# Two inputs transposed by the DMA crossbar, attention in four groups of four heads, and part of its sums as identity matmuls

## The chip, the cores and the metric

The kernel runs on one core of a Trainium2 chip. The time is device microseconds of one execution; where several runs are given, their median is meant. A profile is one execution recorded by the hardware profiler: TensorE (PE, with its weight loads shown apart as PEld), VectorE (DVE), ScalarE (ACT), GpSimd (POOL), SyncE (SP), and the DMA queues. Each engine executes its own list of instructions; semaphores join the lists.

## What is computed

Two independent layers on two inputs of 2048 tokens by 448 features, in bf16, written side by side into one output of 2048 x 896.

```python
# A: a diagonal complex state-space layer, 448 states
Lam_bar = jnp.exp(dt * Lam)
B_bar = ((Lam_bar - 1.0) / Lam)[:, None] * Bmat
Bu = jnp.einsum("bld,pd->blp", x + 0j, B_bar)
for t in range(L):
    h = Lam_bar[None, :] * h + Bu[:, t, :]
y = 2.0 * jnp.einsum("blp,dp->bld", hseq, Cmat).real + x * Dskip[None, None, :]

# B: attention, 16 heads of 28, each token over 8 earlier tokens at distance 0, 2, ... 14
qkv = (x @ wqkv)                      # 448 -> 3 x 16 x 28
logits = jnp.einsum("bhsd,bhswd->bhsw", q, kg) * scale   # -1e9 before the first token
attn = softmax(logits)
o = jnp.einsum("bhsw,bhswd->bhsd", attn, vg)
out_b = o @ wo
```

## The kernel before

A token is 16 p + j: partition p holds 16 consecutive tokens j. So a window reaches at most 14 tokens back, into the partition above; `kd` and `vd` therefore have a halo of 14 tokens in front, filled by a DMA that shifts the last 14 tokens of every partition by one partition (`_halo`, L100).

Part B. `loads` (L54) brings the weights and x in token order. `prep` (L68) reorders the weights on DVE to (d, head) and transposes x on PE, four 128x112 blocks for each j, with a copy on ACT. `qk_proj` and `v_proj` (L104, L115) make k, q and v for all 16 heads: 48 PSUM tiles of 448 columns, four matmuls each; DVE empties k and q, ACT empties v. `attention` (L122) works on all heads at once, on DVE. For each of the eight distances w it multiplies q with the shifted k (7168 elements per partition) and adds over d in a tree of six further additions; softmax follows on 2048 elements per partition; for the values, eight multiplications by the weight and seven additions, done for tokens 0 to 11 and then 12 to 15 (`PV_SPLIT`). `tail` (L175) transposes the result on PE, copies it on DVE, multiplies by wo on PE, copies on ACT and stores from SP, one j at a time.

Part A. `setup` (L254) builds on DVE and ACT the powers of the diagonal, and on POOL the small matrices that apply them: `Mmat` (7 instructions), `Lmat`, `Pmat` (5) and `Gdiag`, in that order. `setup_weights` (L367) makes `Bcat`, the input matrix, by matmuls with `Gdiag`. `main` (L406) transposes x like part B and then has three stages. First level: 16 steps over j, each with 28 matmuls of x and 14 of the former state (`Lmat`), two ACT copies and a store of the state `ht` to `hs` in DRAM. Doubling: seven steps `l2A`, `l2B` across partitions, then `gaA`, `gaB`. Correction and output: for each j the state is read back (`hin`), corrected in PSUM (`coA`, `coB`, 14 matmuls), copied by ACT to `ht`, multiplied by `Ccat` and `Dg` into `y_ps`, copied and stored.

The order on each engine comes from a scheduler in the program's build: it gives every instruction the priority of its place in the program and simulates which is ready, with buffers taken from pools. The program's order is: parameters, loads, `b.prep`, `a.setup`, `b.qk_proj`, `b.v_proj`, `a.setup_c`, `a.setup_weights`, `b.loads2`, `a.main`, `b.attention`. PSUM has six buffers of tag `mm` (projections, all of part A, wo) and two of tag `pt` (transposes). All DMAs but the k halo (ACT) are issued from SP. The list is fixed when the program is built.

Of the kernel before, what the change touches and what calls it, by code (L numbers as in the profile page):

```python
# [9 lines left out]
ACT = mybir.ActivationFunctionType  # L10
ALU = mybir.AluOpType
# [5 lines left out]
D = 448  # L17
T = 16
# [27 lines left out]

class PartB:

    def __init__(self, tc, B_x, B_wqkv, B_wo, out_b, ident, pool, psum):
        self.tc, self.nc = tc, tc.nc  # L50
        self.B_x, self.B_wqkv, self.B_wo, self.out_b = B_x, B_wqkv, B_wo, out_b
        self.ident, self.pool, self.psum = ident, pool, psum

    def loads(self):  # L54
        nc, pool = self.nc, self.pool
        self.wn = pool.tile([KP, KT, 3 * D], bf16, name="wqkv_nat", tag="prod")
        nc.sync.dma_start(self.wn[:], self.B_wqkv.rearrange("(k p) c -> p k c", p=KP))
        self.x_sb = pool.tile([NCH, T, D], bf16, name="xb_sb", tag="xin")
        nc.sync.dma_start(self.x_sb[:], self.B_x[0].rearrange("(p j) d -> p j d", j=T))

    def loads2(self):
        nc, pool = self.nc, self.pool
        self.wo_p = pool.tile([KP, KT, D], bf16, name="wo_p")
        wo_v = self.B_wo.rearrange("(h kt dl) c -> dl h kt c", kt=KT, dl=7)
        for dl in range(7):
            nc.sync.dma_start(self.wo_p[dl * H:(dl + 1) * H, :, :], wo_v[dl])

    def prep(self):  # L68
        nc, pool, V = self.nc, self.pool, self.nc.vector
        self.wp = pool.tile([KP, KT * 3, DH, H], bf16, name="wqkv_p", tag="wp")  # L70
        wn_v = self.wn[:].rearrange("p k (w h d) -> p (k w) d h", w=3, h=H, d=DH)
        wpv = self.wp[:].rearrange("p (k w) d h -> p k w d h", w=3)
        wnv = wn_v.rearrange("p (k w) d h -> p k w d h", w=3)
        V.tensor_copy(wpv[:, :, 0:2], wnv[:, :, 0:2])
        V.tensor_copy(wpv[:, :, 2], wnv[:, :, 2])
        self.xT = pool.tile([KP, KT, T, NCH], bf16, name="xbT_sb", tag="xT")
        for j in range(T):
            pt = self.psum.tile([KP, KT, NCH], bf16, name="pt_x", tag="pt")
            for k in range(KT):
                nc.tensor.transpose(pt[:, k, :], self.x_sb[:, j, k * KP:(k + 1) * KP], self.ident[:])  # L80
            nc.scalar.copy(self.xT[:, :, j, :], pt[:])  # L81
        self.qd = pool.tile([NCH, DH, T, H], bf16, name="qd", tag="qd")
        self.kd = pool.tile([NCH, DH, TJ, H], bf16, name="kd", tag="kd")
        self.vd = pool.tile([NCH, DH, TJ, H], bf16, name="vd", tag="vd")
        zsrc = pool.tile([1, HALO * H], bf16, name="zsrc")
        nc.vector.memset(zsrc[:], 0.0)
        for t_ in (self.kd, self.vd):
            nc.sync.dma_start(t_[0:1, :, 0:HALO, :].rearrange("o d j h -> o d (j h)"),
                              zsrc[:].unsqueeze(1).to_broadcast([1, DH, HALO * H]))

    def _proj(self, j, which):
        nc = self.nc
        ps = self.psum.tile([NCH, DH, H], f32, name="qkv_ps", tag="mm")
        for k in range(KT):
            nc.tensor.matmul(ps[:].rearrange("p d h -> p (d h)"), lhsT=self.xT[:, k, j, :],  # L95
                             rhs=self.wp[:, k * 3 + which].rearrange("p d h -> p (d h)"),
                             start=(k == 0), stop=(k == KT - 1))
        return ps

    def _halo(self, t_, eng):  # L100
        eng.dma_start(t_[1:113, :, 0:HALO, :], t_[0:112, :, T:T + HALO, :])
        eng.dma_start(t_[113:128, :, 0:HALO, :], t_[112:127, :, T:T + HALO, :])

    def qk_proj(self):  # L104
        nc, V = self.nc, self.nc.vector
        scale = DH ** -0.5
        for j in range(T):
            ps = self._proj(j, 1)
            V.tensor_copy(self.kd[:, :, HALO + j, :], ps[:])
        self._halo(self.kd, nc.scalar)  # L110
        for j in range(T):
            ps = self._proj(j, 0)
            V.tensor_scalar(self.qd[:, :, j, :], ps[:], scale, None, op0=ALU.mult)  # L113

    def v_proj(self):  # L115
        nc, V = self.nc, self.nc.vector
        for j in range(T):
            ps = self._proj(j, 2)
            nc.scalar.copy(self.vd[:, :, HALO + j, :], ps[:])  # L119
        self._halo(self.vd, nc.sync)  # L120

    def attention(self):  # L122
        nc, pool, V = self.nc, self.pool, self.nc.vector
        qd, kd, vd = self.qd, self.kd, self.vd
        logits = pool.tile([NCH, W, JH], f32, name="logits", tag="wp")
        for w in range(W):
            off = HALO - DIL * w
            pr = pool.tile([NCH, DH, JH], bf16, name="prod", tag="prod")
            V.tensor_tensor(pr[:], qd[:].rearrange("p d j h -> p d (j h)"),  # L129
                            kd[:, :, off:off + T, :].rearrange("p d j h -> p d (j h)"), op=ALU.mult)  # L130
            V.tensor_tensor(pr[:, 0:14], pr[:, 0:14], pr[:, 14:28], op=ALU.add)  # L131
            V.tensor_tensor(pr[:, 0:7], pr[:, 0:7], pr[:, 7:14], op=ALU.add)
            V.tensor_tensor(pr[:, 0:3], pr[:, 0:3], pr[:, 3:6], op=ALU.add)
            V.tensor_tensor(pr[:, 0:1], pr[:, 0:1], pr[:, 1:2], op=ALU.add)
            V.tensor_tensor(pr[:, 2:3], pr[:, 2:3], pr[:, 6:7], op=ALU.add)
            V.tensor_tensor(logits[:, w, :], pr[:, 0, :], pr[:, 2, :], op=ALU.add)
            if w > 0:
                V.memset(logits[0:1, w, 0:DIL * w * H], -1e9)
        mx = pool.tile([NCH, 4, JH], f32, name="mx", tag="mx")
        V.tensor_tensor(mx[:], logits[:, 0:4, :], logits[:, 4:8, :], op=ALU.max)  # L140
        V.tensor_tensor(mx[:, 0:2], mx[:, 0:2], mx[:, 2:4], op=ALU.max)
        V.tensor_tensor(mx[:, 0:1], mx[:, 0:1], mx[:, 1:2], op=ALU.max)
        V.tensor_tensor(logits[:], logits[:], mx[:, 0:1, :].to_broadcast([NCH, W, JH]), op=ALU.subtract)
        nc.scalar.activation(logits[:], logits[:], ACT.Exp)
        sm = pool.tile([NCH, 4, JH], f32, name="sm", tag="mx")
        V.tensor_tensor(sm[:], logits[:, 0:4, :], logits[:, 4:8, :], op=ALU.add)
        V.tensor_tensor(sm[:, 0:2], sm[:, 0:2], sm[:, 2:4], op=ALU.add)
        V.tensor_tensor(sm[:, 0:1], sm[:, 0:1], sm[:, 1:2], op=ALU.add)
        V.reciprocal(sm[:, 1, :], sm[:, 0, :])
        attn = pool.tile([NCH, W, JH], bf16, name="attn", tag="attn")  # L150
        V.tensor_tensor(attn[:], logits[:], sm[:, 1:2, :].to_broadcast([NCH, W, JH]), op=ALU.mult)
        acc = pool.tile([NCH, DH, T, H], bf16, name="acc", tag="xin")
        self.o_nat = pool.tile([NCH, T, DH, H], bf16, name="o_nat", tag="qd")
        attn4 = attn[:].rearrange("p w (j h) -> p w j h", h=H)
        for (j0, j1) in self.PV_SPLIT:
            n = j1 - j0
            for w in range(W):
                off = HALO - DIL * w
                vv = vd[:, :, off + j0:off + j1, :]
                aa = attn4[:, w:w + 1, j0:j1, :].to_broadcast([NCH, DH, n, H])  # L160
                if w == 0:
                    V.tensor_tensor(acc[:, :, j0:j1, :], aa, vv, op=ALU.mult)
                else:
                    tmp = pool.tile([NCH, DH, T, H], bf16, name="pv_tmp", tag="prod")
                    V.tensor_tensor(tmp[:, :, 0:n, :], aa, vv, op=ALU.mult)  # L165
                    if w < W - 1:
                        V.tensor_tensor(acc[:, :, j0:j1, :], acc[:, :, j0:j1, :], tmp[:, :, 0:n, :], op=ALU.add)  # L167
                    else:
                        V.tensor_tensor(self.o_nat[:, j0:j1].rearrange("p j d h -> p d j h"),  # L169
                                        acc[:, :, j0:j1, :], tmp[:, :, 0:n, :], op=ALU.add)  # L170
            self.tail(j0, j1)

    PV_SPLIT = ((0, 12), (12, 16))

    def tail(self, j0, j1):  # L175
        nc, pool = self.nc, self.pool
        if j0 == 0:
            self.oT = pool.tile([KP, KT, T, NCH], bf16, name="oT_sb", tag="xT")
# [385 lines left out]
```

## Time and profile before

| | us |
|---|---|
| time, median of 3 runs (lowest to highest) | 213.12 (212.28 to 213.27) |
| span of the profiled execution, first to last instruction | 211.4 |
| DVE busy | 181.0 (86%) |
| PE busy / weight loads | 160.4 (76%) / 117.4 |
| ACT busy | 100.2 (47%) |
| POOL busy | 28.1 (13%) |
| PE waits for x of part B | 18.5 |
| projections on PE, in the chain | 29.29 to 62.62 |
| part A: first level to the last output copy | 69 to 176.8 |

The span and the time are of different executions; the profiled execution's own time is its span and what lies around it, so a sum is made against the span and then carried over. A group's busy time counts all of its instructions; it is on the path only where another engine waits for it. The chain that ended last, followed back from the last instruction, gives the path: until 62.6 us it consists of the x load, transposes and projections, then of part A on PE until about 123 us, and from there to the end of attention on DVE with the last tail.

### The profile page before, as it was taken

The page shows a single profiled execution, that of the slowest core. Times are in us where ns is not written, and L with a number is a line of the kernel's source. Part 1 is how long each engine was busy: PE and PEld are TensorE (multiplying, and loading weights), DVE is VectorE, ACT ScalarE, POOL GpSimd, SP SyncE. Part 2 cuts the span into 40 slices and gives each one's busy share as a digit, 9 for nine tenths or more (in the row PEclk, how much of TensorE's full clock was granted, in tenths as well). Part 3 has the DMA queues.
Part 4 walks back from the last instruction along what each step waited for, and adds up shares of the span by engine and source line. Part 5 has one row for each costly group of instructions (what it writes and reads, how often), then busy time and mean ns, then how long its engine had stood idle before and what let it go on. Part 6 is the DMA issues. An engine that isn't in the chain of part 4 may idle for free.

```text
span 211.4 us, 4117 instructions
## 1 busy us (share of the span) xinstructions
PE 160.4 (76%) x1709; PEld 117.4 (56%) x1709; DVE 181.0 (86%) x197; ACT 100.2 (47%) x193; POOL 28.1 (13%) x35
## 2 busy tenths in 40 slices
PE   0004999999997799999995763998888883297773
PEld 0003765555567799999994652565555551154441
DVE  0359998888929999999999996999999999999950
ACT  2053792002689993344337796344455541024432
POOL 2000899991000000000000000000000000000000
PEclk9999999999999999999999998599999999569999
DMA  1599940485508515422231011134354411012212
GB/s 0 103 351 289 244 108 0 108 192 161 212 2 209 95 47 171 164 106 90 87 118 59 3 43 43 47 110 129 92 137 126 112 43 43 0 43 72 83 65 87
DMA packets 23836, 22.17 MB, mean 105 GB/s; under 512 B 11786, under 2 KB 23114, under 8 KB 23562
## 3 DMA queue, kind: packets, MB, share of 16 engines
q1 hardware_dynamic: 20231, 20.32, 32.9%
q10 hardware_dynamic: 3587, 1.59, 3.2%
q8 instruction: 13, 0.21, 0.5%
q14 instruction: 5, 0.04, 0.1%
HBM read 11.36 MB, written 7.34 MB: 88 GB/s over the span
## 4 chain that ended last, share of the span: by engine, by line
PE 46%; DVE 33%; ACT 8%; DMA 6%; issue 3%; SPq 2%; ACTq 0%; DVEq 0%
PE qkv_ps L95 18%; DVE pv_tmp L165 13%; DVE acc L167 10%; PE l1A L392 7%; DMA xb_sb<-in_B_x_dram 6%; PE l1B L392 5%; PE wo_ps L188 3%; PE pt_x L80 3%; DVE oT_sb L185 2%; PE pt_x L415 2%; DVE o_nat L169 2%; ACT Bcat L379 2%; PE l1A L397 1%; PE l1A L399 1%; ACT Ccat L250 1%
## 5 line engine op out<-in xcount | busy, mean ns | idle before, releaser
L95 PE MATMUL qkv_ps<-wqkv_p,xbT_sb 112*128 112x448 bf16 x192 | 40.1, 361 | 0.0
L129 DVE TENSOR_TENSOR prod<-qd,kd 128x7168 bf16<-128x7168 bf16 x8 | 30.7, 3840 | 0.1
L165 DVE TENSOR_TENSOR pv_tmp<-attn,vd 128x5376 bf16<-128x5376 bf16 (+1 forms) x14 | 28.3, 2021 | 0.3
L95 PEld LDWEIGHTS <-xbT_sb 112*128 112x128 bf16 x192 | 18.8, 100 | 15.5
L392 PEld LDWEIGHTS <-Bcat 112*128 112x128 bf16 x448 | 26.2, 98 | 0.0
L167 DVE TENSOR_TENSOR acc<-acc,pv_tmp 128x5376 bf16<-128x5376 bf16 (+1 forms) x12 | 24.3, 2024 | 0.3
L80 PE MATMUL pt_x<-ident,xb_sb 128*112 128x128 bf16 x64 | 7.8, 266 | 18.8 <-DMA xb_sb<-in_B_x_dram 18.5
L483 ACT CAST ya<-y_ps 128x448 bf16<-128x448 f32 x16 | 8.5, 531 | 23.4 <-issue 18.8
L191 ACT CAST yb<-wo_ps 128x448 bf16<-128x448 f32 x16 | 8.5, 532 | 23.3 <-PE wo_ps L188 23.3
L80 PEld LDWEIGHTS <-xb_sb 128*112 128x112 bf16 x64 | 7.5, 173 | 21.1 <-DMA xb_sb<-in_B_x_dram 18.5
L402 ACT CAST ht<-l1A 128x512 bf16<-128x512 f32 x16 | 9.4, 587 | 19.2 <-issue 17.0
L119 ACT CAST vd<-qkv_ps 128x448 bf16<-128x448 f32 x16 | 8.4, 536 | 20.8 <-PE qkv_ps L95 20.7
L392 PE MATMUL l1A<-xaT_sb,Bcat 112*128 112x128 bf16 x256 | 18.1, 219 | 0.0
L188 PE MATMUL wo_ps<-wo_p,oT_sb 112*128 112x448 bf16 x64 | 15.0, 382 | 3.8 <-DVE oT_sb L185 3.7
L131 DVE TENSOR_TENSOR prod<-prod 128x3584 bf16<-128x3584 bf16 x8 | 16.2, 2025 | 0.3
L343 POOL TENSOR_TENSOR Mmat<-Dm,Scat 128x896 bf16<-128x896 f32 x7 | 11.6, 1688 | 19.3 <-DVE Scat L335 19.3
L392 PE MATMUL l1B<-xaT_sb,Bcat 112*128 112x128 bf16 x192 | 14.2, 219 | 0.0
L81 ACT COPY xbT_sb<-pt_x 112x512 bf16<-112x512 bf16 x16 | 8.8, 587 | 7.3 <-PE pt_x L80 7.3
L184 PE MATMUL pt_o<-ident,o_nat 128*112 128x128 bf16 x64 | 5.8, 244 | 8.3 <-DVE o_nat L169 8.3
L113 DVE TENSOR_SCALAR qd<-qkv_ps 128x448 bf16<-128x448 f32 x16 | 10.0, 625 | 2.1
L188 PEld LDWEIGHTS <-oT_sb 112*128 112x128 bf16 x64 | 6.0, 103 | 10.1 <-DVE oT_sb L185 5.0
L469 PEld LDWEIGHTS <-ident 128*128 128x128 bf16 x112 | 11.3, 101 | 0.0
(206 smaller groups left out, 360.9 us busy)
## 6 DMA issues: line engine op xcount, KB each, us to landing
hs<-ht SPq DMA_DIRECT2D x16, 224.0 KB, 1.9
hin<-hs SPq DMA_DIRECT2D x16, 224.0 KB, 2.7
xb_sb<-in_B_x_dram SPq DMA_DIRECT2D x1, 1792.0 KB, 12.3
xa_sb<-in_A_x_dram SPq DMA_DIRECT2D x1, 1792.0 KB, 7.9
out_dram<-ya SPq DMA_DIRECT2D x16, 112.0 KB, 1.7
out_dram<-yb SPq DMA_DIRECT2D x16, 112.0 KB, 1.7
kd<-kd ACTq DMA_DIRECT2D x1, 1372.0 KB, 9.1
vd<-vd SPq DMA_DIRECT2D x1, 1372.0 KB, 9.4
```

What stands on the lines that cost most here:

```text
L80: nc.tensor.transpose(pt[:, k, :], self.x_sb[:, j, k * KP:(k + 1) * KP], self.ident[:])
L95: nc.tensor.matmul(ps[:].rearrange("p d h -> p (d h)"), lhsT=self.xT[:, k, j, :], rhs=self.wp[:, k * 3 + which].rearrange("p d h -> p (d h)"),
L113: V.tensor_scalar(self.qd[:, :, j, :], ps[:], scale, None, op0=ALU.mult)
L129: V.tensor_tensor(pr[:], qd[:].rearrange("p d j h -> p d (j h)"), kd[:, :, off:off + T, :].rearrange("p d j h -> p d (j h)"), op=ALU.mult)
L131: V.tensor_tensor(pr[:, 0:14], pr[:, 0:14], pr[:, 14:28], op=ALU.add)
L165: V.tensor_tensor(tmp[:, :, 0:n, :], aa, vv, op=ALU.mult)
L167: V.tensor_tensor(acc[:, :, j0:j1, :], acc[:, :, j0:j1, :], tmp[:, :, 0:n, :], op=ALU.add)
L188: nc.tensor.matmul(ps[:], lhsT=oT[:, kt, j, :], rhs=self.wo_p[:, kt, :], start=(kt == 0), stop=(kt == KT - 1))
L343: eng.tensor_tensor(out_tile, Dm[:].unsqueeze(1).unsqueeze(1).to_broadcast([NCH, n, 2, PL]), scal.unsqueeze(3).to_broadcast([NCH, n, 2, PL ...
L392: nc.tensor.matmul(reg(m), lhsT=self.Bcat[:, k, m, :], rhs=self.xT[:, k, j, :], start=(k == 0 and m in (0, MA)), stop=(not has_prev and k ...
L402: nc.scalar.copy(ht[:, 0:MA, :], psA[:])
L469: nc.tensor.matmul(reg(m), lhsT=ident[:], rhs=hin[:, m, :], start=(m in (0, MA)), stop=False, skip_group_check=True)
```

## The change

x of both parts is no longer loaded in token order and transposed by PE. `_load_xT` issues crossbar transposes from SP (four DMAs for B, two for A), straight from DRAM. Since 448 is not a multiple of 128, two consecutive tokens j make seven blocks of 128 rows; the fourth block belongs half to each, and `_ktiles` names for every j the three whole blocks and the half one. All weights that multiply x (`w7`, `Bcat`, `Dg`) have seven row blocks to match. Every product has four contraction steps for each j, as before.

Attention runs in four groups of four heads. `proj(g)` makes q, k and v of one group, with all copies on ACT; both halo DMAs are on SP, and POOL clears the first partition. `attention(g)` works on two halves of eight tokens. One DVE multiplication covers all eight distances (7168 elements); one addition folds 112 columns to 56, one from 56 to 28 writes seven slices, and PE adds these seven by matmuls with the identity into the PSUM tile `lg`, over a mask that another identity matmul puts there first. Softmax reads PSUM: two reductions instead of trees. For the values, one multiplication of 7168 elements covers all distances, one addition folds eight to four, and PE sums the four distances and transposes in one step (`po`, the products as stationary operand, identity as moving one). ACT copies `po` to `oT`; the wo product of `tail` has one contraction step per group.

PSUM now has four buffers of tag `mm` and four of tag `bp` (projections, `lg`, `po`). The small parameters are loaded from ACT, part A's matrices and wo from POOL. `a.main`, without its transposes, comes last in the program.

```diff
+def _load_xT(nc, dst, x, parts=4):
+    rows = x.rearrange("(p j) d -> p (j d)", j=T)
+    step = NB * NPAIR // parts
+    for i in range(parts):
+        nc.sync.dma_start_transpose(dst[:, i * step:(i + 1) * step, :],
+                                    rows[:, i * step * 128:(i + 1) * step * 128])
...
+    def proj(self, g):
...
+        for j in range(0, T, 4):
+            pp = [self.psum.tile([NCH, 2, 2, HG, DH], f32, name="qk_ps", tag="bp") for _ in range(2)]
+            self._project(...)
+            for o in range(2):
+                nc.scalar.copy(kd[:, HALO + j + o:HALO + j + o + 3:2], pv[:, :, 1])
+                nc.scalar.activation(qd[:, j + o:j + o + 3:2], pv[:, :, 0], ACT.Copy, scale=scale)
+        self._halo(kd)
...
+    def attention(self, g):
+        lg = self.psum.tile([NCH, 2, nx], f32, name="lg", tag="bp")
+        nc.tensor.matmul(lg, lhsT=self.ident[:], rhs=self.mask, start=True, stop=False, ...)
+        for a in range(2):
+            pr = pool.tile([NCH, n, GW], bf16, name="prod", tag="prod", bufs=2)
+            V.tensor_tensor(pr, qv.unsqueeze(1).to_broadcast(...), self._windows(kd, a * JHALF), op=ALU.mult)
+            V.tensor_tensor(pr[:, :, 0:56], pr[:, :, 0:56], pr[:, :, 56:112], op=ALU.add)
+            V.tensor_tensor(red[:].rearrange("p d n h -> p n d h"), pr[:, :, 0:28], pr[:, :, 28:56], op=ALU.add)
+            for d in range(7):
+                nc.tensor.matmul(lg[:, a], lhsT=self.ident[:], rhs=red[:, d], start=False, stop=(d == 6), ...)
+        V.tensor_reduce(mx[:], lv.rearrange("p a w x -> p a x w"), axis=AX.X, op=ALU.max)
...
+        for a in range(2):
+            tmp = pool.tile([NCH, W, JHALF, GW], bf16, name="pv_tmp", tag="prod", bufs=2)
+            V.tensor_tensor(tmp, attn[:, a] (repeated over d), self._windows(vd, a * JHALF), op=ALU.mult)
+            V.tensor_tensor(tmp[:, 0:4], tmp[:, 0:4], tmp[:, 4:8], op=ALU.add)
+            for j in range(0, JHALF, 4):
+                po = self.psum.tile([GW, 4, NCH], f32, name="po", tag="bp")
+                for i in range(4):
+                    for w in range(4):
+                        nc.tensor.matmul(po[:, i], lhsT=tmp[:, w, j + i, :], rhs=self.ident[:], ...)
+                nc.scalar.copy(self.oT[:, g, a * JHALF + j:a * JHALF + j + 4, :], po[:])
+            if g == NG - 1:
+                self.tail(a * JHALF, (a + 1) * JHALF)
...
-            return psum.tile(shape, dtype, name=name, tag=tag, bufs=(6 if tag == "mm" else 2))
+            return psum.tile(shape, dtype, name=name, tag=tag, bufs=4)
...
-    b.loads()
+    b.load_w(0)
+    b.load_x()
+    b.consts()
     a.loads()
-    b.prep()
+    b.load_w(1)
+    b.proj(0)
+    a.load_x()
     a.setup()
-    b.qk_proj()
-    b.v_proj()
     a.setup_c()
     a.setup_weights()
-    b.loads2()
+    b.attention(0)
+    b.proj(1)
+    b.load_w(2)
+    b.load_wo()
+    b.attention(1)
+    b.proj(2)
+    b.load_w(3)
+    b.attention(2)
+    b.proj(3)
+    b.attention(3)
     a.main()
-    b.attention()
```

## The prediction

> **What bounds the kernel now.** I read first the busy shares and the span in slices, then the chain that ended last, then single stretches, then the groups with shapes kept apart.
>
> ```profile
> PE   0004999999997799999995763998888883297773
> DVE  0359998888929999999999996999999999999950
> POOL 2000899991000000000000000000000000000000
> PEclk9999999999999999999999998599999999569999
> PE 46%; DVE 33%; ACT 8%; DMA 6%; issue 3%; SPq 2%; ACTq 0%; DVEq 0%
> ```
>
> From slice 12 on PE and VectorE (DVE) are both busy: DVE works on attention, which in this kernel needs PE only at its end, while PE runs all of part A. The chain is mostly PE until 123 us and DVE after that. So the time rests on an overlap of two long jobs. These stretches show it:
>
> ```profile
> 69.00:111.00 42.00, 41.11 (x711) 40.50 (x711) 40.77 (x41) 22.86 (x47) 0.00 (x0) 1.00 0.33 109
> 111.00:124.00 13.00, 8.57 (x131) 7.48 (x129) 12.60 (x14) 9.86 (x20) 0.00 (x0) 1.00 0.07 25
> 124.00:177.00 53.00, 42.12 (x399) 27.72 (x395) 50.16 (x25) 27.26 (x54) 0.00 (x0) 0.94 0.31 90
> ```
>
> (start:end, length, then busy us and instructions of PE, weight loads, DVE, ACT, POOL; clock, DMA share, GB/s.) They are part A's first level, doubling steps, and correction with output. DVE is busy for 103.5 of these 108 us.
>
> **The change, part by part.** The diff alone doesn't give the order on PE; the built program does. PE executes it front to back:
>
> ```
> proj(0); lg mask; Ccat transposes; lg(0); 98 ps_b; 64 po(0)
> proj(1); lg mask; 4 wo; lg(1); 64 po(1)
> proj(2); lg mask; 4 wo; lg(2); 64 po(2)
> proj(3); lg mask; 4 wo; lg(3); po(3) mixed with the rest of wo
> then all of part A: l1, l2, ga, co and y
> ```
>
> Two things follow. (1) The projection of group g+1 stands behind po(g), whose operand is DVE's last result of group g: DVE has nothing to do until PE, ACT and the halo DMA have made the next q and k. (2) Part A stands behind the last wo. Its tiles share four PSUM buffers with wo, and four wo tiles are opened in group 1 and closed only in group 3. The overlap above is gone.
>
> The durations:
>
> ```profile
> L129 DVE TENSOR_TENSOR prod<-qd,kd 128x7168 bf16<-128x7168 bf16 x8 | 30.7, 3840 | 0.1
> L131 DVE TENSOR_TENSOR prod<-prod 128x3584 bf16<-128x3584 bf16 x8 | 16.2, 2025 | 0.3
> L132 DVE TENSOR_TENSOR prod<-prod 128x1792 bf16<-128x1792 bf16 x8 | 8.7, 1092 | 0.3
> L169 DVE TENSOR_TENSOR o_nat<-acc,pv_tmp 128x5376 bf16<-128x5376 bf16 x1 | 3.0, 2958 | 0.0
> L141 DVE TENSOR_TENSOR mx<-mx 128x512 f32<-128x512 f32 x1 | 0.7, 692 | 0.0
> L149 DVE RECIPROCAL sm<-sm 128x256 f32<-128x256 f32 x1 | 1.8, 1753 | 0.0
> ...
> L402 ACT CAST ht<-l1A 128x512 bf16<-128x512 f32 x16 | 9.4, 587 | 19.2 <-issue 17.0 <-PE l1A L399 1.2 <-ACT ht L403 1.0
> L343 POOL TENSOR_TENSOR Lmat<-Dm,Shl 128x1792 bf16<-128x1792 f32 x1 | 3.2, 3189 | 0.6 <-DVE Shl L340 0.6
> ```
>
> *DVE in one group.* Logits: two multiplications of 7168 (3.84), two additions of 3584 (2.03), two of 1792 (1.09): 13.9. Softmax: lg matmuls behind the last of these 1.7 (seven of 256 columns, half clock); five steps on 512 elements: max, subtract, sum, scale at 0.69 and the exponential on ACT at 0.6 with 0.2 of hand-over; the reciprocal of 64, 0.56 (between 0.20 at 7 and 1.75 at 256): 5.8. Values: two 3.84 and two 2.03: 11.7. Together 31.5, or 126 for four. Before, the same rows and the 16 tail copies (418 ns each) make most of the 181 us of busy DVE, so DVE does lose some 50 us of work. Two forms are not in the trace: the addition writing runs of four (8x), and the multiplication by a weight repeated over d, read in runs of four (8x). L169 wrote runs of 16 at the price of L167, so I take the two-element rate; the other end is half rate, 8 x 0.9 + 8 x 3.8 = 38 us more. Below nothing I exclude: no two-input row is faster per element.
>
> *From a group's last addition to the next multiplication.* po: 64 matmuls of 128 columns, half of which may start 2 us early. In part A one takes 0.056 us (42 in the 2.35 us of a first-level step; in the chain l1A starts at 104.31 and 106.66); at half clock 0.11; what remains after the addition is 1.8 to 4.8, I take 2.8. q and k: 64 matmuls of 224 columns; L95 ran 134 of 448 columns in 25.35 us, so 0.095 each, 6.1. The last copies on ACT 1.4 (three of 224 elements, about 0.36 by L402 and L403). Halo: two issues of 0.65 and the landing, by the 224 KB store of hs (1.9 us) for 343 KB: 3.1. Sum 13.4, between 11 and 17. It comes three times, one of them inside group 0's figure. The v projection and its halo fall under the next logits (13.9 us) and cost nothing.
>
> The clock row first: 1.00 while PE is dense, 0.55 in the stretch from 180 to 190 us, where PE waits. The Trainium skill, "TensorE: Matmul & The Clock Gate", Part 1, says that an idle window of some 3.4 us halves the clock and that as long a busy one restores it. By that rule po and the start of each projection run at half clock, some 1.7 us a group; at full clock each bubble would be 1 us shorter than mine. The row agrees in kind; the sum doesn't need the rule.
>
> *Start.* DVE's first multiplication is now ahead of part A's setup in its queue. It waits for x transposed (SP, four DMAs behind eight weight loads, issued from about 8 us; before, x was issued at 6.2), the last projection and copies (3 us), and the k halo, which stands on SP behind the first half of A's x. No row shows a crossbar transpose. Bounds: as a plain load, 7.9 us for these 1792 KB (xa_sb), gives a start near 23; as 256-byte pieces at the rate of the k halo's 448-byte ones (3587 packets in 9.2 us, so 18.4 for 7168) 38 with half of A's x in front. I take 32.
>
> A price only a page states: "VectorE: DVE Perf Modes", The three transpose paths, gives 1309 ns for one 128x128 crossbar transpose. One after another, 56 would be 73 us for B's x alone, and the sum would pass 420; the page on DMA ("DMA: Bandwidth & Descriptors", Latency and other measured facts) has 261 GB/s, some 7 us, by which it would be near 341.
>
> *Group 0.* Setup's results come only between its logits: Scat after 13.9 + 4 of small steps = 18. POOL then has seven Mmat, Lmat, five Pmat, and Gdiag last: 12 x 1.69 + 2 x 3.19 = 26.7 back to back. DVE and POOL obstruct each other here (a copy of 7 elements, L327, took 3.2 us beside POOL); big DVE steps may push POOL by 0 to 15, I take 7. The 98 ps_b matmuls need Gdiag and stand in front of po(0): 14 copies on ACT, 8. Then po 4.4, and as above 6.1 + 1.4 + 3.1. Sum 75 from the first to the second group's multiplication. DVE alone would be free after some 42: in this group POOL, not DVE, is the bound.
>
> *Tail.* The last wo and its copies: 16 tiles with two yb buffers, each held for a copy (0.53) and a store (1.7 to landing, issue and hand-over 0.4), so 1.3 a tile; with the four PSUM buffers about 21 us from DVE's end to A's first matmul. Between 12 (PE alone) and 23.
>
> *Part A.* Its work on PE is unchanged, without the x transposes. First level 16 x 2.35 less the first step's missing part: 36.8; to the end of ga 12.4 (111.36 to 123.73); 16 steps of 2.86 (the ya copies at 170.53 and 173.39), 1.6 ahead and 2.5 for the last copy and store: 49.9. Sum 99. Four instead of six PSUM buffers: a step uses two or three and frees them within 1.1 us; nothing, covered by the next step's 28 x-matmuls (1.57 us); without cover up to 1 us a step, 16.
>
> ```profile
> 170.53 0.53 ACT L483 CAST ya<-y_ps 128x448 bf16<-128x448 f32 x1 [1.45 <-issue]
> ...
> 173.39 0.53 ACT L483 CAST ya<-y_ps 128x448 bf16<-128x448 f32 x1 [1.45 <-issue]
> ```
>
> **Sum.** 32 + 75 + 2 x (31.5 + 13.4) + 31.5 + 21 + 99 = 348.3 us of span. The profiled execution has 211.4, the median of the three times is 213.12, so 1.7 lie around it: 350 us, 64% more than before.
>
> **The rivals.** *PE fills its waits* (the other sign). If PE took the next projection, ps_b and part A while it waits for DVE, the serial 99 us of A, 3 x 13.4 of bubbles and some 24 of group 0's wait would fall under DVE: 350 - 163 = 187. It decides from 137 us hidden on; A alone hidden leaves 251, still slower. For it: DVE's work shrinks. Against it: the order above, and the trace, where PE stood still 3.8 us for ht_1807 although the next step's co matmuls, whose hin was issued at 84.33, stood behind it in the queue. 0.03, with 0.05 for 240 to 300 by a part of it.
>
> *Runs of four at half rate.* 350 + 38 = 388; with slow additions alone 357. For it: no row has such short runs; against it: L169. 0.10.
>
> *Slow transposes.* At twice the packet price 18 more for B's x and 9 for A's half in front of the halo: 377 or above. For it: the first multiplication is bare to it; against it: later groups are not touched. 0.12.
>
> **How the numbers follow.** The serial order with my prices has 0.70 (318 to 372: start 23, bubbles 11, POOL not pushed, tail 12 at one end; start 38, bubbles 17, POOL pushed 15 at the other, not all at once). The range must leave out no more than 2 in 10, so it takes in half rate and moderately slow transposes: 315 to 392. A measurement here tells 0.5% from no change; only the first rival's full form ends below 213: faster 0.03, within 0.5% 0.01, slower 0.96.
>
> **What would show it.** Right: DVE idle some 13 us before each group's first multiplication, released by the halo's DMA; PE's first l1 matmul after the last wo, some 99 us before the end, with DVE empty in that stretch; Gdiag as releaser of ps_b near 80 us; DVE busy near 135. Wrong: l1 beside DVE work, multiplications of 7.6 us, a first multiplication after 50 us.

## The result, and the profile after

The changed kernel takes 377.38 us (median of four runs, 375.36 to 378.96) against 212.70 us for the kernel before on the same chip: a ratio of 1.777, 95% interval [1.767, 1.787]. The prediction was 350 us with a range of 315 to 392. The three waits that it named are what the profile shows; the sum was 28.6 us of span too small. The profiled execution's span is 376.9 us, and the steps below are made against it.

The slices and the chain of the changed kernel:

```profile
PE   0019411000597030880307903057799996788885
DVE  0000399996002959309594096960000000000000
POOL 7810105999700100000000000000000000000000
PEclk9999655555599555695556965559999998999999
...
PE 33%; DVE 26%; DMA 13%; issue 11%; ACT 10%; POOL 6%; SPq 0%; ACTq 0%; DVEq 0%
```

One slice is 9.4 us. Up to slice 26 PE and VectorE take turns: where one has a 9, the other has 0 or 1. From slice 27 on VectorE is empty, and PE does all of part A alone. Before, the two were busy side by side from slice 12 to the end. The chain names each of the engines in turn, and 13% of it are transfers.

Two stretches show both halves of this (start:end, length, then busy us and instructions of PE, weight loads, DVE, ACT, POOL; clock, DMA share, GB/s):

```profile
220.00:240.00 20.00, 3.30 (x14) 1.83 (x13) 15.57 (x12) 0.63 (x1) 0.00 (x0) 0.50 0.00 0
...
280.00:300.00 20.00, 20.00 (x332) 18.34 (x330) 0.00 (x0) 7.73 (x16) 0.00 (x0) 1.00 0.37 122
```

In the first, a group's logits and softmax, PE works 3.3 of 20 us, at half clock; in the second, part A's first level, VectorE does nothing. Before, 41 of 42 us of the same level ran beside 40.8 us of VectorE.

VectorE's first multiplication of each group, in order of time (start, duration, engine, line, tiles; in brackets the idle time before it and its releaser):

```profile
43.80 3.89 DVE L188 TENSOR_TENSOR prod<-qd,kd 128x7168 bf16<-128x7168 bf16 x1 [15.12 <-ACT Ccat L310]
...
120.37 7.69 DVE L188 TENSOR_TENSOR prod<-qd,kd 128x7168 bf16<-128x7168 bf16 x2 [29.77 <-DMA kd<-kd]
...
168.83 7.69 DVE L188 TENSOR_TENSOR prod<-qd,kd 128x7168 bf16<-128x7168 bf16 x2 [15.17 <-DMA kd<-kd]
...
217.46 7.69 DVE L188 TENSOR_TENSOR prod<-qd,kd 128x7168 bf16<-128x7168 bf16 x2 [15.34 <-DMA kd<-kd]
```

Groups 1 to 3 wait for the halo of their own k, and that for the projection behind the last group's po. Group 0's row names ScalarE's copy of Ccat; in three other runs below the same multiplication is released by its halo too. With VectorE's end at 250.7 us, part A's first matmul at 269.86 and the end at 376.9, the span splits as the prediction split it:

| step | predicted, us | measured, us |
|---|---|---|
| first multiplication | 32 | 43.8 |
| group 0, to the second group's multiplication | 75 | 76.6 |
| groups 1 and 2, each | 44.9 | 48.5, 48.6 |
| group 3, to VectorE's end | 31.5 | 33.3 |
| tail of wo | 21 | 19.1 |
| part A | 99 | 107.0 |

VectorE's busy time is 135.3 us (135 was predicted), 46 us less than before: the change does take that work off VectorE. It then pays for it with waits.

### The profile page after: what moved, and what is told of

Read it like the earlier page. It is cut to its first block, busy times and chain, and to the rows that moved or that the text cites. A ratio compares the mean times of both kernels' runs of the same rounds, so it can differ in the third digit from the quotient of the medians.

```text
span 376.9 us, 5199 instructions
## 1 busy us (share of the span) xinstructions
PE 192.7 (51%) x2195; PEld 149.5 (40%) x2195; DVE 135.3 (36%) x104; ACT 115.1 (31%) x254; POOL 60.9 (16%) x68
## 4 chain that ended last, share of the span: by engine, by line
PE 33%; DVE 26%; DMA 13%; issue 11%; ACT 10%; POOL 6%; SPq 0%; ACTq 0%; DVEq 0%
DVE pv_tmp L216 7%; PE qk_ps L127 6%; PE po L226 5%; DMA w<-in_B_wqkv_dram 5%; PE l1A L454 4%; DVE prod L188 4%; DVE prod L191 4%; POOL Pmat L403 4%; DMA out_dram<-yb 3%; PE l1B L454 3%; PE lg L197 3%; DMA kd<-kd 3%; ACT ht L526 2%; DMA xbT_sb<-in_B_x_dram 2%; DVE red L193 2%
## 5 line engine op out<-in xcount | busy, mean ns | idle before, releaser
L188 DVE TENSOR_TENSOR prod<-qd,kd 128x7168 bf16<-128x7168 bf16 x8 | 30.9, 3888 | 75.4 <-DMA kd<-kd 60.3
L226 PE MATMUL po<-ident,pv_tmp 128*112 128x128 bf16 x256 | 22.4, 268 | 42.9 <-DVE pv_tmp L221 42.9
L127 PEld LDWEIGHTS <-xbT_sb 128*128 128x128 bf16 x384 | 27.8, 100 | 31.0 <-DMA xbT_sb<-in_B_x_dram 26.9
L226 PEld LDWEIGHTS <-pv_tmp 128*112 128x112 bf16 x256 | 21.8, 174 | 45.0 <-DVE pv_tmp L221 44.4
L127 PE MATMUL qk_ps<-w,xbT_sb 128*128 128x224 bf16 x192 | 22.9, 273 | 26.9 <-DMA xbT_sb<-in_B_x_dram 26.9
L216 DVE TENSOR_TENSOR pv_tmp<-attn,vd 128x7168 bf16<-128x7168 bf16 x8 | 33.6, 4245 | 0.3
L454 PEld LDWEIGHTS <-Bcat 128*128 128x128 bf16 (+1 forms) x448 | 25.8, 97 | 3.4 <-issue 1.3
L530 PE MATMUL y_ps<-Ccat,ht 128*128 128x448 bf16 x112 | 24.0, 354 | 5.9 <-ACT ht L526 5.9
L454 PE MATMUL l1A<-xaT_sb,Bcat 128*128 128x128 bf16 (+1 forms) x256 | 24.6, 219 | 1.1 <-ACT yb L240 0.6
L454 PE MATMUL l1B<-xaT_sb,Bcat 128*128 128x128 bf16 x192 | 20.7, 218 | 0.0
L221 DVE TENSOR_TENSOR pv_tmp<-pv_tmp 128x3584 bf16<-128x3584 bf16 x8 | 18.8, 2389 | 0.0
L464 ACT CAST ht<-l1A 128x512 bf16<-128x512 f32 x16 | 9.4, 585 | 24.6 <-issue 19.1
```

What stands on the lines that cost most here:

```text
L127: nc.tensor.matmul(out, lhsT=self.xT[r0:r1, c, :], rhs=w(r0, r1, b), start=(first and i == 0), stop=False, skip_group_check=True)
L188: V.tensor_tensor(pr[:].rearrange("p (w j) c -> p w (j c)", w=W), qv.unsqueeze(1).to_broadcast([NCH, W, JHALF * GW]), self._windows(kd, a ...
L216: V.tensor_tensor(tmp[:].rearrange("p w j (d h) -> p w j d h", h=HG), attn[:, a].rearrange("p (w j) h -> p w j h", w=W).unsqueeze(3).to_br ...
L221: V.tensor_tensor(tmp[:, 0:4], tmp[:, 0:4], tmp[:, 4:8], op=ALU.add)
L226: nc.tensor.matmul(po[:, i], lhsT=tmp[:, w, j + i, :], rhs=self.ident[:], start=(i == 0 and w == 0), stop=(w == 3), skip_group_check=True)
L454: nc.tensor.matmul(reg(m), lhsT=self.Bcat[r0:r1, b, m, :], rhs=self.xT[r0:r1, c, :], start=(i == 0 and m in (0, MA)), stop=(not has_prev a ...
```

## The experiments

The theory: three orders make the time, each on its own. Part A stands behind wo because both take PSUM tiles from one pool; the projection of a group stands behind the attention of the one before it on PE; and group 0 waits for the last of GpSimd's matrices. The rivals are that VectorE, PE or the transfers set the time however the work is ordered. Each edit below is on the changed kernel unless it says otherwise, and the ratios are to the kernel before, run beside it.

### wo's tiles from the other PSUM pool

```
-            ps = self.psum.tile([NCH, D], f32, name="wo_ps", tag="mm")
+            ps = self.psum.tile([NCH, D], f32, name="wo_ps", tag="bp")
```

> Edit: the wo tiles take their PSUM buffers from tag bp instead of mm; nothing else. Theory (order: part A stands behind the last wo because four early wo tiles hold A's buffers): the built order now has part A's matmuls between the lg and po of groups 1 to 3, and after the last wo only the last four output steps, some 12 us. A's 107 us shrink to that; attention moves by under 10 us. 282 to 297 us, about 85 less than 377. Rival (PE's own amount of work, at half clock, is the bound): what A takes is taken from attention; 360 to 380 us.

Measured: 278.47 us, ratio 1.310 [1.303, 1.318], 3.5 us below the expected range. One word takes 99 us off. Slices of this run:

```profile
PE   0001944220000089999898999677899898899984
...
DVE  0100008999999000069599009869703968930000
```

From slice 15 on PE is busy through VectorE's groups. Between VectorE's last instruction and the end lie 32 us, where the changed kernel has 126. The first l1 matmul comes at 117.87 us, ahead of the second group's attention, instead of at 269.86. So the order of wo and part A was no need of the data; four buffers that wo's open tiles held made it.

### The projection ahead of the attention before it

```
-    b.attention(0)
     b.proj(1)
     b.load_w(2)
+    b.attention(0)
     b.load_wo()
...
```

(and the same for groups 1 and 2)

> Edit: in the program the projection of group g+1 stands ahead of the attention of group g; nothing else. Theory (DVE waits about 15 us before each group because the next projection stands behind po): the waits before groups 2 and 3 go from 15 to under 4 us, and in front of group 1 the part behind po goes (10 to 12 us). 335 us, between 330 and 345. Rival (DVE waits for the prod buffers, which po frees, not for the projection): the waits become 7 us (po), 350 to 357. Rival (PE work is the bound): no gain, 377.

Measured: 334.6 us, ratio 1.577 [1.569, 1.585]. VectorE's order of time in this run:

```profile
107.39 7.70 DVE L188 TENSOR_TENSOR prod<-qd,kd 128x7168 bf16<-128x7168 bf16 x2 [17.69 <-PE po L226]
...
141.10 7.69 DVE L188 TENSOR_TENSOR prod<-qd,kd 128x7168 bf16<-128x7168 bf16 x2 [1.87 <-PE po L226]
...
174.51 7.69 DVE L188 TENSOR_TENSOR prod<-qd,kd 128x7168 bf16<-128x7168 bf16 x2 [1.56 <-PE po L226]
```

The 15 us in front of groups 2 and 3 shrink to under 2, and what is left is released by po, which frees the product's buffer, not by the halo. In front of group 1 there remain 17.7: by the next run's measure that is GpSimd's Gdiag, which this edit leaves where it was. The bubbles are priced as the prediction priced them, and they are an order, not a dependence.

### Gdiag ahead of GpSimd's other matrices

The four statements that make gs and Gdiag move from behind Pmat to in front of Lmat; nothing else changes.

```
+        self.Gdiag = pool.tile([NCH, 2 * NM, NCH], bf16, name="Gdiag", tag="gdiag")
+        G.tensor_tensor(self.Gdiag[:], ident[:] (repeated), gs[:] (repeated), op=ALU.mult)
         self.Lmat = pool.tile([NCH, 2 * NM, 2, PL], bf16, name="Lmat")
...
```

> One edit on the changed kernel: Gdiag, the only one of GpSimd's matrices that group 0 waits for, is asked for ahead of the others; three of Mmat and Lmat still come before it in the built program, so it ends near 74 us and not at 98.6. Theory (group 0's 76.6 us are GpSimd's queue ahead of Gdiag and nothing else): Bcat's matmuls are then done beside VectorE's values, which end at 90.6 as before, and the second group starts one ordinary waiting stretch of 15.2 us later, at 106 and not 120.4: 377 - 14.5 = 363 (358 to 368). Rival (a later matrix, or VectorE itself, holds the group): 372 to 380.

Measured: 358.89 us, ratio 1.688 [1.676, 1.700], so -18.5 where -14.5 was expected. In the changed kernel PE waits for Gdiag until 98.6 (first fence); in this run Gdiag ends at 71.1 (second fence; GpSimd in order of time):

```profile
98.62 0.26 PE L436 MATMUL ps_bA<-Gdiag,bXY 128*128 128x128 bf16 x1 [38.62 <-POOL Gdiag L419]
```

```profile
67.93 3.18 POOL L411 TENSOR_TENSOR Gdiag<-ident,gs 128x1792 bf16<-128x1792 bf16 x1 [0.38 <-DVE gs L409]
71.07 16.15 POOL L403 TENSOR_TENSOR Mmat<-Dm,Scat 128x896 bf16<-128x896 f32 x4
87.19 10.05 POOL L403 TENSOR_TENSOR Pmat<-Dm,Scat 128x896 bf16<-128x896 f32 x5
```

The second group's first multiplication comes at 102.19 us, not 120.37. Its wait falls from 29.8 us to 13.1, about what groups 2 and 3 wait: what group 0 waited beyond the ordinary bubble was GpSimd's queue. 1.7 us of the gain is an earlier first multiplication (42.10 us), which the edit doesn't explain. The thirteen other matrices are wanted by part A alone, much later; four of them still stand ahead of Gdiag in this run.

### The parameters' arithmetic before the first projection

```
+    a.powers()
     a.loads_params()
     b.load_w(0)
     b.load_x()
     b.consts()
+    a.setup()
     a.loads()
     b.load_w(1)
     b.proj(0)
     a.load_x()
-    a.setup()
```

(powers() holds setup()'s thirteen memsets of kv, moved to the front)

> Edit: part A's setup stands in front of the first projection in the program, and the constants of the powers are set first on POOL. Theory (in group 0 POOL's chain to Gdiag holds ps_b, and ps_b holds po(0) and the next projection): Scat comes near 31 us instead of 60, Gdiag near 60 instead of 98.6, and the second group's first multiplication at 90 to 95 instead of 120. 347 to 353 us. Rival (DVE and POOL obstruct each other wherever they meet, so the sum of their work stays): under 10 us gained, 368 to 377.

Measured: 364.56 us, ratio 1.714 [1.706, 1.723]; a miss of some 14 us. The expected part came: from the first to the second group's multiplication 50.5 us instead of 76.6. But the first multiplication moved from 43.8 to 56.51:

```profile
56.51 7.70 DVE L188 TENSOR_TENSOR prod<-qd,kd 128x7168 bf16<-128x7168 bf16 x2 [25.90 <-POOL kd L138]
```

The memset that clears the k halo is GpSimd's, and it now stood behind GpSimd's matrices (to 55.08 us), with some of the loads that GpSimd issues. I had moved a step past one queue and not looked at what else that queue carries: 12.7 of the 26 us were given back. A later run, below, clears the halos first.

### The transposes of B's x first on SP

The prediction's start was 11.8 us short. In the changed kernel (SP's queue in order of time) the eight loads of weights in front of the transposes were not through by 8 us:

```profile
7.12 0.68 SPq L100 DMA_DIRECT2D w<-in_B_wqkv_dram  x1
10.66 0.53 SPq L101 DMA_DIRECT2D w<-in_B_wqkv_dram  x1
17.95 11.14 SPq L68 DMA_TRANSPOSE xbT_sb<-in_B_x_dram  x4
```

SP's wait in front of the transposes was for weights still on their way (6.7 us at the longest). So I put the transposes first:

```
+    b.load_x()
+    b.load_w(0)
     a.loads_params()
-    b.load_w(0)
-    b.load_x()
```

> Edit: x of part B is the first transfer that SP issues, then the weights, then ACT's parameters in the program; nothing else. Theory (of the 43.8 us to the first multiplication, the first 18 are spent on waiting for earlier small transfers, the crossbar itself takes about 11): the transposes start before 2 us, the first multiplication comes 6 to 14 us earlier; 363 to 371 us. Rival (the crossbar transposes are what is slow, or the halo behind part A's x): they start early but the first multiplication moves by under 3 us; 374 to 378.

Measured: 398.23 us, ratio 1.874 [1.864, 1.885]. Both expectations fell: 21 us slower than the changed kernel. The issue of the four transposes now held SP's queue for 37.5 us, the median one landed 21.9 us after its issue (5.9 in the changed kernel), and the first multiplication came at 65.1. Beside them ran GpSimd's large loads (bXY: 392 KB pieces, landing in 21 us instead of 9.8) and ScalarE's ten loads of parameters. Two runs were to take away one of these at a time. In the first, bXY and C are loaded by SP behind the weights (nc.gpsimd.dma_start becomes nc.sync.dma_start in loads()):

> The transposes of B_x go first on SP, as in the run that did only this, and the ten GpSimd loads of bXY, cre_nat and cim_nat are issued by SP behind the first weights, so that beside the transposes only the ten small parameter loads of ScalarE are under way. Theory 1 (the large loads of GpSimd slow the transposes): the four are issued in 8 to 12 us and land in about 6 each, PE starts near 21 and the first multiplication near 38, against 43.8 in the changed kernel: 367 to 374 us. Theory 2 (the element-wise parameter loads of ScalarE slow them): issue takes some 37 us again, the first multiplication stays near 65, time 390 to 402.

In the second, GpSimd's loads stay, and a.loads_params(), which holds ScalarE's loads of parameters, moves behind b.proj(0) in the program:

> The transposes of B_x go first on SP, the loads of GpSimd stay where they are, and the ten parameter loads of ScalarE stand behind the evictions of the first projection. Theory 1 (the loads of GpSimd slow the transposes): the four take some 30 us or more to issue, landing above 15 us each, as before with all three queues. Theory 2 (the parameter loads do): issue in 8 to 12 us, landing near 6. The time tells less, since the parameters themselves come late here and with them Scat and the matrices of GpSimd: 375 to 390 under theory 2, 395 to 415 under theory 1.

Measured: 360.08 us, ratio 1.696 [1.685, 1.706], for the first, 7 us below its range; 397.85 us, ratio 1.874 [1.859, 1.888], for the second. SP's queue in the transposes-first run, then with bXY behind, then with a.loads_params() moved:

```profile
0.75 37.52 SPq L68 DMA_TRANSPOSE xbT_sb<-in_B_x_dram  x4
```

```profile
0.75 12.94 SPq L68 DMA_TRANSPOSE xbT_sb<-in_B_x_dram  x4
```

```profile
0.75 36.40 SPq L68 DMA_TRANSPOSE xbT_sb<-in_B_x_dram  x4
```

The second edit did not take ScalarE's loads away. In the built queue they still come first, issued from 0.74 to 33.4 us, beside the transposes as before, and VectorE has two of the parameters long before the first projection starts at 45.94 (second run, VectorE in order of time):

```profile
7.84 0.17 DVE L323 CAST lre<-lre_raw 128x7 f32<-128x7 bf16 x1 [6.87 <-DMA lre_raw<-in_A_Lambda_re_dram]
...
33.05 0.17 DVE L323 CAST lim<-lim_raw 128x7 f32<-128x7 bf16 x1 [24.84 <-DMA lim_raw<-in_A_Lambda_im_dram]
```

So that run repeats the transposes-first run. Its 397.85 us lies in the range of the theory of GpSimd's loads because nothing changed, and it tests neither theory. The first run does: there too ScalarE's ten loads ran beside the transposes (issued from 0.75 to 11.3 us), and the four took 12.94. ScalarE's loads alone don't make them slow; GpSimd's large loads are needed for it. Whether those do it without ScalarE's loads beside them, no run shows. A few of GpSimd's loads don't do it: in the changed kernel its two C loads of 392 KB were on their way for the first 2 and 4 us of the transposes' issue, its four of 98 KB ran beside it, and it took 11.14 us. In the run with the early arithmetic it took 8.16 us; there three of GpSimd's ten loads were issued before it, from 2.6 to 4.9 us, and the other seven from 50.1 us on.

With bXY out of the way PE starts at 17.54 us instead of 26.88, the parameters land in 5 to 8 us (ldt 16.2 in the changed kernel), Scat is there at 22.98 instead of 59.84, and Gdiag ends at 61.7 instead of 98.6. The first multiplication comes 5.3 us earlier than in the changed kernel, the second group's 17.3 (103.12); the 12 us in group 0 are what I had not counted on. Whether the loads disturb by their size alone, or because GpSimd issues them, these runs don't separate: the first edit changed the queue and the moment together.

### Do the gains add?

The first two edits together, and then with the arithmetic early and the halos of two groups cleared ahead of it (b.tiles(0) and b.tiles(1), called before a.setup(), allocate q, k and v and clear the halos):

> Both edits at once: the output projection takes its PSUM from the other pool, and each projection stands ahead of the attention before it. If the two costs were independent, -99 and -43 from 377 would give 235. Theory: they are not; both gains fill the same waits of PE, and part A cannot begin before Gdiag (98 us) in either, so after 98 us PE has some 150 us of work left (177 of the run with the other pool, less what lies ahead): 258 to 275. Rival (independent): 230 to 245.

> Both edits and the parameters' arithmetic ahead of the first projection, with the halo rows of the first two groups cleared, and all loads of GpSimd issued, ahead of its matrices, which is what the run with the early setup lacked. GpSimd's matrices then run from about 24 to 51 us, first multiplication near 44, four groups of some 34.5 us each (PE and VectorE then need about 31.5 each a group) to about 185, then the output projection and some eleven output steps of part A: 218 to 242. If the early matrices are worth nothing once the other two edits are made: 258 to 275, as without.

Measured: 273.45 us, ratio 1.288 [1.283, 1.293]; and 247.66 us, ratio 1.163 [1.156, 1.171], above its range of 218 to 242. They don't add. With wo freed, the projections' order brings VectorE's end from 243 to 204 us and the end of the kernel only 5 us forward, because after Gdiag (98 us) PE is nearly full (busy for 94 of the 106 us up to VectorE's end): what VectorE no longer waits for, part A no longer fills. Early matrices are worth 26 us on top of that, since they let PE begin. My estimate for the second was short because the matrices ran from 33.5 to 72 us and not from 24 to 51: the last small steps on VectorE that Lmat needs came only at 33 us, and big multiplications of VectorE then fell beside GpSimd.

### A version that comes close

Everything that paid, with Gdiag first and the transposes first with bXY behind them:

> Everything that paid, together: output projection from the other PSUM pool, each projection ahead of the attention before it, the transposes of B_x first with the large loads behind them on SP, the parameters' arithmetic ahead of the first projection with Gdiag first on GpSimd. PE then starts at 17.5 us and has some 178 us of work (182 and 177 in the last two runs), VectorE 136. Theory (PE is the bound once nothing stands in its queue): 17.5 + 178 + some 12 of waits at half clock and between groups + 3 at the end = 210 (203 to 222), level with the kernel before at 212. Rival (the output steps of part A left behind the last group, 8 of 16 in the built order, cannot be filled, and VectorE's four groups set the end): 38.5 + 4 x 33.5 = 172.5, then 14.6 + 24 + some 10 = 222 to 235.

Measured: 228.52 us, ratio 1.076 [1.071, 1.081], by the rival's number. The theory's engine was right all the same: PE's busy time is 177.6 of 225.8 us, and after VectorE's end it is busy for 17 to 20 of each 20 us. Of its 48 idle us, 17 lie before its start and 7.6 are a wait for the second group's weights, which stood on SP behind ten large loads. The next run mends that:

```
     b.load_w(0)
+    b.load_w(1)
     a.loads_params()
...
-        nc.sync.dma_start(t_[1:113, 0:HALO], t_[0:112, T:T + HALO])
+        nc.scalar.dma_start(t_[1:113, 0:HALO], t_[0:112, T:T + HALO])
...
```

> On top of everything that paid: the second group's weights are loaded ahead of bXY on SP, and the halo copies of k and v are issued by ScalarE behind its own evictions, not by SP behind eighteen loads. Theory (PE is the bound, 177.6 us of work and 48 idle, of which 7.6 were the wait for those weights): the 7.6 go, the first multiplication comes near 30 and not at 39: 228.5 - 7.6 = 221 (214 to 228). Rival (the end is set by the last group on VectorE and part A's last steps behind it, so that the start of PE counts little but the earlier first multiplication counts in full): 228.5 - 9 = 219; and if the loads of bXY, now later, hold up Bcat's matmuls, no gain: 226 to 232.

Measured: 219.97 us, ratio 1.036 [1.032, 1.040]. Theory and rival forecast 221 and 219 here, so the time doesn't decide between them, and the first multiplication came at 35.73 us, not near 30. The weights' and the halos' shares aren't separated. The last one gives VectorE one addition back:

```
             V.tensor_tensor(tmp[:, 0:4], tmp[:, 0:4], tmp[:, 4:8], op=ALU.add)
+            V.tensor_tensor(tmp[:, 0:2], tmp[:, 0:2], tmp[:, 2:4], op=ALU.add)
...
-                    for w in range(4):
+                    for w in range(2):
```

> On top of the run before, one of the two halvings that the change gave to PE goes back to VectorE: the values are added once more over tokens (128 x 1792 elements out, eight times, some 1.2 us each by half of the 2.39 of the addition before it), and po sums two terms and not four (128 matmuls less, some 55 ns each at full clock). Theory (PE is the bound): -7 of PE's work, +9.6 of VectorE's, which has slack: 221 - 7 = 214 (207 to 221), level with the kernel before at 212. Rival (VectorE's groups are the bound, whatever PE does): +9.6 on the run before, near 230.

Measured: 214.28 us, ratio 1.010 [1.006, 1.013]. The page's busy row and slices of this run:

```profile
PE 168.6 (79%) x2067; PEld 131.0 (62%) x2067; DVE 137.2 (65%) x112; ACT 112.7 (53%) x254; POOL 54.1 (25%) x58
...
PE   0007989179799989979988975769989888999963
DVE  0345004999059999968999986998995899300000
```

PE lost 7.6 us of work (176.2 in the run before), VectorE gained 6.9, and the time fell by 5.7. So in this version PE sets the time, and not VectorE, though it still idles 44 of the 212.5 us of the span, 17 of them before its start. Moving this one sum from VectorE to PE, as the change does, costs time here, and moving it back gains; the change's other moves weren't undone. The kernel before has PE busy for 160.4 us, and it is still 1.0% faster than this best version. No run beat it.

## Why the prediction was right, point by point

*The order on PE, both parts (1) and (2).* Shown, each by the run that undoes it alone: 99 us and 43 us. The rival "PE fills its waits" was right to be named as a question of order and not of work: with wo's tiles elsewhere PE does fill them. Its figure for part A alone hidden, 251, was too low against 278.5: it is 350 - 99, so group 0's wait and the bubbles are in it. The run took 98.9 us off, so the price of 99 held, and the difference is what the sum of 350 itself lacked.

*Start, 32 us: mis-sized, 43.8.* The term that failed is "issued from about 8 us". SP's eight loads took until 11 us, and the transposes were issued at 17.95. The price of the transposes themselves was better: issue of the four took 11.14 us, PE began at 26.88 with the first piece, and it took up the last one at 33.50 without a wait, 15.5 us after the first issue, so B's x was there sooner than the 18.4 us by packets. The rival of slow transposes was wrong for the changed kernel, yet not for the chip: first in the queue, beside large loads, they took 36 to 38 us. The page's 1309 ns for one 128x128 transpose (the Trainium skill, "VectorE: DVE Perf Modes", The three transpose paths) would make 73 us of these 56; 11.14 us of issue in the changed kernel is 0.20 us each, so as a price for many in a row it does not hold here. No run reached the 7 us that came from the 261 GB/s of "DMA: Bandwidth & Descriptors", Latency and other measured facts: the shortest issue was 8.16 us.

*Group 0, 75 us: right to 1.6, its mechanism shown by the run with Gdiag first.* Inside it GpSimd was pushed by 11.7 us (60.14 to 98.57 against 26.7 back to back), within the 0 to 15 allowed, where I took 7. That the sum comes so close is partly luck: GpSimd's 4.7 us more are partly made up by 1.7 less to Scat, 0.7 less of po and 0.5 less for Bcat.

*The bubble, 13.4 us: 15.2 and 15.3.* The mis-sized term is po. In front of group 3 VectorE ends at 202.1 and po at 206.4: 4.3 us remained, not 2.8; the 64 matmuls took 6.13 us there and 3.74 in group 0, right behind the Bcat matmuls. The first stretch above has the clock at 0.50 while VectorE works. So the rule that the prediction weighed (the Trainium skill, "TensorE: Matmul & The Clock Gate", Part 1) names what happens here, and its half clock was the end of my 1.8 to 4.8 to take; I had taken 2.8, nearer the other. The projection was 6.3 us (6.1). The halo took 0.7 more than priced, the last copies 0.3 less.

*VectorE in one group, 31.5 us: 33.3 in group 3.* All steps are as priced but the sum in the softmax, 1.01 us and not 0.69, and one wait that I did not see: red has one buffer, so the second addition waits 1.74 us for the first half's lg matmuls (at half clock), and the softmax waits another 1.74, which I had. The two unknown forms, by shape and with means in ns:

```profile
L216 DVE TENSOR_TENSOR pv_tmp<-attn,vd 128x7168 bf16<-128x7168 bf16 x8 | 33.6, 4245 | 0.3
L188 DVE TENSOR_TENSOR prod<-qd,kd 128x7168 bf16<-128x7168 bf16 x8 | 30.9, 3888 | 75.4 <-DMA kd<-kd 60.3 <-ACT Ccat L310 15.1
...
L193 DVE TENSOR_TENSOR red<-prod 128x1792 bf16<-128x1792 bf16 x8 | 8.7, 1089 | 5.2 <-PE lg L197 5.2
```

The addition that writes runs of four takes 1.09 us, as one that writes long runs. The multiplication by the repeated weight has a mean of 4.25 only because its two in group 0 ran beside GpSimd (10.55 us for both); in the last run, where GpSimd is done by then, its mean is 3888 ns, the same as the plain one's in the changed kernel. The rival of half rate fell.

*Tail, 21 us: 19.1.* Right, and by the two yb buffers as priced: ScalarE's copies waited ten times for the store before, 9.3 us in all, in the view of waits.

*Part A, 99 us: 107.0.* The first level took 40.8 us instead of 36.8. "A step's 28 x-matmuls (1.57 us)" was mis-sized, since I held part A's work on PE unchanged: the new tiles of transposed x have halves of 64 rows, and the change of the row count costs. PE in order of time, changed kernel:

```profile
285.60 0.39 PE L454 MATMUL l1A<-xaT_sb,Bcat 128*128 128x128 bf16 x4
...
286.00 0.39 PE L454 MATMUL l1A<-xaT_sb,Bcat 128*128 128x128 bf16 x4
286.22 0.33 PE L454 MATMUL l1B<-xaT_sb,Bcat 128*128 128x128 bf16 x3
286.48 0.39 PE L454 MATMUL l1A<-xaT_sb,Bcat 64*128 64x128 bf16 x4
286.71 0.33 PE L454 MATMUL l1B<-xaT_sb,Bcat 64*128 64x128 bf16 x3
```

The start of seven matmuls after the start of the seven before is 0.40 us within one kind (285.60 to 286.00), and 0.48 across the change to 64 rows (286.00 to 286.48). With the change back, the 28 take 1.77 us against 1.56 before, when each had 112 rows. That is 3.4 of the 4.0 us; no run undoes it alone. The output steps took 3.03 us each and not 2.86 (2.7 us in all), with a 64-row matmul in each, and the doubling steps with Ga 14.3 and not 12.4, at a clock of 0.88; 0.7 us came back at the ends. Four PSUM buffers instead of six cost nothing, as said: PE was busy for 40.29 of the first level's 40.8 us.

The sum of the misses: 11.8 + 1.6 + 3.6 + 3.7 + 1.8 - 1.9 + 8.0 = 28.6.

## What to carry to other kernels

A change that moves work to an engine is priced by the order that the built program gives that engine: three orders, each a line or a word to undo, made 99, 43 and 18 us here, each alone (they don't add), while the work that the change took off VectorE was 46 us. An accumulating PSUM tile that stays open across stages holds its buffer, and whatever shares the pool stands behind it. A queue carries more than the step that one moves: halo memsets, loads and weights stood behind moved work in three of these runs, and each time the gain shrank or turned.

## What the runs showed of the hardware

- Four transposes of 448 KB, the first in SP's queue: 12.94 us of issue with only ScalarE's small loads and three of 98 KB beside them, 37.52 and 36.40 us beside GpSimd's large loads as well, which themselves took 20 to 21 us to land instead of 10. Later in the queue they took 8.16 us (early arithmetic) and 11.14 us (changed kernel). The whole traffic was 111 and 112 GB/s while the two slow ones were issued, little less than the 123 beside the 12.94; it was 196 right after those and 220 around the changed kernel's transposes, with other loads beside them.
- VectorE and GpSimd slow each other both ways. In the changed kernel Pmat took 3.13 us a piece beside VectorE's large multiplications, against 1.69 before, and two of those multiplications took 10.55 us instead of 7.69.
- A matmul stream that changes between 128 and 64 rows loses about 0.1 us at each change (above).
